# A fused attention and feed-forward kernel: the sign of a decoded weight made on ScalarE, the first batches' normalisations taken from ScalarE to VectorE

## The chip, the core and the metric

The kernel runs on one core of a Trainium2 chip. The metric is the device time of one execution in microseconds (us); lower is better. The engines are named as the profile names them: PE is TensorE (PEld its weight loads), DVE is VectorE, ACT is ScalarE, POOL is GpSimd, SP is SyncE, which here issues nearly all transfers from memory. A name such as L214 is line 214 of the kernel before. In the changed kernel all lines behind L213 have a number that is lower by one.

## The reference

Eight batches with eight heads of a causal attention with a window of 128 and a bias that grows with distance, then a feed-forward layer over all 4608 rows:

```python
scores = scale * np.matmul(q, k.transpose(0, 1, 3, 2))
bias = slopes[:, None, None] * (-np.abs(rel).astype(np.float32))[None, :, :]
mask = (rel >= 0) & (rel < window)
scores = np.where(mask, scores + bias[None], -1000000000.0)
scores = scores - np.max(scores, axis=-1, keepdims=True)
attn = np.exp(scores)
attn = attn / (np.sum(attn, axis=-1, keepdims=True) + 1e-09)
...
h = x @ w_in
g = h * (1.0 / (1.0 + np.exp(-1.702 * h)))
return (g @ w_out).astype(np.float32)
```

Here x is the attention's output laid out as 4608 rows of 512. The weights w_in (512 by 2048) and w_out (2048 by 512) are 64-bit floats.

## The kernel before

**Attention** is worked in units. The batches 0 and 1 are cut into three parts of rows (0 to 256, 256 to 512, 512 to 576) for each pair of heads: these 24 "whole" units (class WholeUnit) work in full float32. The batches 2 to 7 are cut into units that split their operands into a rounded part and a remainder. A unit passes through a pipeline of ticks: load its q, k and v, scores on PE (L325 for whole units), bias and running minimum on DVE (L352), exponentials and row sums on ACT (L375), the reciprocal of the sums on DVE (L393 and L394), the normalisation of the up to four pieces of the unit (L400 and L403), transposes on PE (L420) with copies out of PSUM (L428), and the product with v (L477), copied into the tile xf of a chunk (L486). The scores of one tick need PSUM tiles that DVE's L352 of the tick before has read, and the transposes need all normalised pieces.

**Normalisation of a whole unit.** A string of letters gives the engine of each piece: "PPVA" for the four early units (batch 0, rows 0 to 256), "PAPA" for the others; P is POOL, V is DVE, A is ACT. A unit of 64 rows has two pieces and uses the first two letters. In all there are 36 pieces on ACT, 40 on POOL and 4 on DVE.

**Feed-forward.** The rows are cut into 18 chunks of 256, and for each chunk 16 steps f run over slices of 128 of the 2048 hidden units: 12 products into h_ps (L553), tanh on ACT (L558), the gate on DVE (L559), a rounded part on ACT (L562) and a remainder on POOL (L563), and 6 products into acc (L572). The chunks 0 and 1 run their first steps while the weights are still being decoded: the jobs are chunk 0 with 8 steps, chunk 1 with 16, chunk 0 with its last 8, then the rest.

**Decoding.** A block of 128 by 512 weights arrives as 64-bit words (tile rw, 512 KB, one transfer each, 32 in all, two for each f), and is turned into float32 once. Of each word `top` is the upper half (sign, 11 bits of exponent, 20 of mantissa) and `low` the lower. ACT reads `top` as a float32 and scales it by 2 to the power -112 (L211), which lowers the exponent field so that after a shift left by three the exponent is that of a float32; DVE shifts `low` right by 29 in place (L212), shifts the scaled word left by 3 and joins the three bits from `low` (L213), which drops the sign; then DVE joins the sign bit of `top` (L214). ACT makes the rounded part (L217) and POOL the remainder (L218). The tile `wc` in which the word is made has three buffers, so the L211 of a block waits for the L218 of three blocks earlier. The first eight blocks' instructions are pinned to the program's order.

**What sets the order.** Each engine works through its own list in order. A scheduler sets the lists when the program is built, from its own model of the durations, except where the code pins an order (the transfers on SP's queue, the idle products that open the program at L189, the first eight decodings). Decoding and attention are fed into the feed-forward steps by counters (`owed`, `credit`) that do not depend on measured times. The transfers of weights stand in one queue with those of q, k and v, and these wait for free buffers.

Of the kernel before, what the change touches and what calls it, by code (L numbers as in the profile page):

```python
# [8 lines left out]
F32 = mybir.dt.float32  # L9
# [4 lines left out]
AF = mybir.ActivationFunctionType  # L14
ALU = mybir.AluOpType
# [127 lines left out]
def tile_kernel(ctx: ExitStack, tc: tile.TileContext, q0, k0, v0, qT, kT, v, w_in, w_out, out):  # L143
    nc = tc.nc
# [58 lines left out]
    def decode(st, name, pin=lambda ins: ins):  # L203

        words = st.bitcast(I32).rearrange("p (m two) -> p m two", two=2)
        top, low = words[..., 1], words[..., 0]
        c = ffn.tile([P, 512], I32, name="wc", tag="o", bufs=3)

        pin(nc.scalar.activation(c.bitcast(F32), top.bitcast(F32), AF.Copy, scale=2.0 ** -112))  # L211
        pin(nc.vector.tensor_scalar(low, low, 29, None, ALU.logical_shift_right))  # L212
        pin(nc.vector.scalar_tensor_tensor(c, c, 3, low, ALU.logical_shift_left, ALU.bitwise_or))  # L213
        pin(nc.vector.scalar_tensor_tensor(c, top, -0x80000000, c, ALU.bitwise_and, ALU.bitwise_or))  # L214
        w = c.bitcast(F32)
        res = const.tile([P, 2, 512], F32R, name=name, tag=name)
        pin(nc.scalar.copy(res[:, 0], w))  # L217
        pin(nc.gpsimd.tensor_tensor(res[:, 1], w, res[:, 0].bitcast(F32), ALU.subtract))  # L218
        return res
# [167 lines left out]
    def normal(u):  # L387
        u.rec = att.tile([P, 4], F32, name="rec", bufs=3)
        if u.whole:
            rows, ne = u.blocks[0][1], len(u.p)  # L390
        else:
            rows, ne = u.blocks[0].rows, len(u.blocks)
        nc.vector.tensor_scalar(u.rec[:rows, :ne], u.sums[:rows, :ne], 1e-9, None, ALU.add)  # L393
        nc.vector.reciprocal(u.rec[:rows, :ne], u.rec[:rows, :ne])  # L394
        if u.whole:
            engines = "PPVA" if u.early else "PAPA"
            for _, live, e in u.p:
                rec = u.rec[:rows, e:e + 1]
                if engines[e] == "A":
                    nc.scalar.activation(live, live, AF.Copy, scale=rec)  # L400
                else:
                    on = nc.gpsimd if engines[e] == "P" else nc.vector
                    on.tensor_scalar(live, live, rec, None, ALU.mult)  # L403
            return
        for e, b in enumerate(u.blocks):
            live = b.p[:rows, b.live:b.end]
            nc.vector.tensor_scalar(live, live, u.rec[:rows, e:e + 1], None, ALU.mult)  # L407
# [202 lines left out]
    def tick():  # L610

        nonlocal ticks
        n = ticks

        def stage(k, *steps):
            u = units[n + k] if 0 <= n + k < len(units) else None
            for step in steps:
                if u:
                    step(u)

        stage(1, split_q)
        stage(-2, flip, split_v)
        stage(0, load_v)
        stage(-1, biased)
        stage(1, split_rest)
        stage(-1, exponents)
        stage(-1, normal)
        stage(-2, high, low)
        stage(0, scores)
        stage(-3, mix)  # L630
        if n + 1 < len(units) and units[n + 1] and loads:
            load(loads.pop(0))
        ticks += 1
# [11 lines left out]
    def decode_next():  # L645
        nonlocal halves
        g, ws = halves // 2, (w1, w2)[halves % 2]

        pin = [tc.keep_in_program_order] if halves < PINNED else []
        ws[g] = decode(ws[g], f"w{1 + halves % 2}_{g}", *pin)  # L650
        halves += 1
# [123 lines left out]
```

## Time and profile before

| what | value |
|---|---|
| median of 3 runs | 1074.23 us (1074.23 to 1074.42) |
| profiled execution, from its first to its last instruction | 1072.5 us |
| mean granted PE clock | 0.991 |
| PE busy | 1053.5 us, 98% |
| DVE busy | 687.3 us, 64% |
| ACT busy | 595.2 us, 56% |
| POOL busy | 610.8 us, 57% |

The profile gives no other time of its own execution than this span, 1.7 us below the median of the runs. Its shares are means over stages with different limits. The kernel has a first stage of about 107 us, in which the weights arrive and are decoded beside the whole units, and a long one behind it, in which PE works through prepared operands; the views by stretch of time tell them apart.

### The profile page before, as it was taken

To read this page: it belongs to the slowest core of one execution; us is meant where nothing else is said; L and a number is where in the kernel's file an instruction comes from. 1 tells how busy PE (TensorE), PEld (TensorE's weight loads), DVE (VectorE), ACT (ScalarE), POOL (GpSimd) and SP (SyncE) were. 2 spreads that over 40 slices of the span, in tenths; PEclk is the share of its full clock that TensorE was granted. 3 is DMA by queue.
4 is the path that set the end of the run, shared out by engine and by line. 5 is a ranking of instruction groups with operands and counts; after the bars stand their busy time and mean duration, and the time that the engine had idled before them with its cause. 6 is when DMAs were issued, how large, how long until landed. Compare 5 with 4: busy or idle time off the path is not lost.

```text
span 1072.5 us, 21419 instructions
## 1 busy us (share of the span) xinstructions
PE 1053.5 (98%) x7041; PEld 931.5 (87%) x7041; DVE 687.3 (64%) x2149; ACT 595.2 (56%) x1811; POOL 610.8 (57%) x863
## 2 busy tenths in 40 slices
PE   9888999999999999999999999999999999999998
PEld 5656777899999999999999999999999999999987
DVE  6899843647896777654667668767877687413121
ACT  6869954546665565444555555655665556322222
POOL 3669954556675666554656557656666565323222
PEclk9889999999999999999999999999999999999999
DMA  8861112312223132202222213222222221000000
GB/s 309 305 231 54 44 30 75 83 38 77 75 80 85 51 86 75 62 16 67 58 76 54 70 53 90 75 60 71 82 65 85 57 77 28 20 2 20 1 21 20
DMA packets 88110, 78.45 MB, mean 73 GB/s; under 512 B 36800, under 2 KB 79296, under 8 KB 88000
## 3 DMA queue, kind: packets, MB, share of 16 engines
q1 hardware_dynamic: 82240, 67.14, 21.7%
q10 hardware_dynamic: 5760, 9.96, 2.5%
q8 instruction: 55, 0.90, 0.4%
q14 instruction: 55, 0.45, 0.1%
HBM read 67.63 MB, written 9.44 MB: 72 GB/s over the span
## 4 chain that ended last, share of the span: by engine, by line
PE 92%; DVE 4%; ACT 1%; DMA 1%; issue 0%; POOL 0%; SPq 0%; DVEq 0%; POOLq 0%; ACTq 0%
PE acc L572 37%; PE h_ps L553 37%; PE s_ps L335 5%; PE x_ps L500 5%; PE t_ps L443 4%; PE x_ps L477 1%; DVE wc L214 1%; DVE wc L213 1%; PE t_ps L420 1%; PE sb_ps L325 1%; DVE rw L212 1%; ACT pb L375 1%; PE s_ps L325 1%; DMA rw<-w_out 1%; DVE pb L352 0%; PE acc L189 0%
## 5 line engine op out<-in xcount | busy, mean ns | idle before, releaser
L563 POOL TENSOR_TENSOR gl<-g,gh 128x256 fp32r<-128x256 f32 x288 | 219.7, 763 | 284.1 <-ACT gh L562 220.0
L553 PE MATMUL h_ps<-xh,w 128*128 128x256 f32 x2304 | 370.2, 284 | 1.5 <-DVE g L559 1.0
L553 PEld LDWEIGHTS h_ps<-xh,w 128*128 128x128 f32 x2304 | 329.2, 189 | 33.2 <-DVE g L559 2.0
L572 PE MATMUL acc<-w,gh 128*128 128x512 f32 x1152 | 326.7, 401 | 0.5 <-ACT gh L562 0.5
L558 ACT ACTIVATE g<-h_ps 128x256 f32<-128x256 f32 x288 | 110.0, 382 | 237.5 <-PE h_ps L553 213.3
L559 DVE SCALAR_TENSOR_TENSOR g<-g,h_ps 128x256 f32<-128x256 f32 x288 | 119.4, 415 | 190.6 <-ACT g L558 189.3
L572 PEld LDWEIGHTS acc<-w,gh 128*128 128x128 f32 x1152 | 196.9, 189 | 28.2 <-ACT gh L562 1.1
L553 PE MATMUL h_ps<-xl,w 128*128 128x256 f32 x1152 | 196.1, 281 | 0.0
L562 ACT CAST gh<-g 128x256 fp32r<-128x256 f32 x288 | 116.5, 405 | 137.7 <-DVE g L559 127.0
L572 PE MATMUL acc<-w,gl 128*128 128x512 f32 x576 | 187.6, 401 | 0.1
L553 PEld LDWEIGHTS h_ps<-xl,w 128*128 128x128 f32 x1152 | 165.2, 189 | 6.7 <-issue 0.3
L313 POOL TENSOR_TENSOR K<-rk,K 128x384 fp32r<-128x384 f32 (+1 forms) x120 | 109.1, 909 | 75.0 <-ACT Q L293 14.3
L382 ACT ACTIVATE pb<-pb,mins 128x256 f32<-128x256 f32 (+2 forms) x216 | 105.0, 487 | 40.7 <-DVE mins L363 39.6
L572 PEld LDWEIGHTS acc<-w,gl 128*128 128x128 f32 x576 | 92.6, 189 | 10.5 <-issue 2.2
L407 DVE TENSOR_SCALAR pb<-pb,rec 128x256 f32<-128x256 f32 (+2 forms) x216 | 94.5, 473 | 3.3
L312 POOL TENSOR_TENSOR Q<-rq,Q 64x256 fp32r<-64x256 f32 (+1 forms) x120 | 82.8, 690 | 22.3 <-DVE g L559 3.3
L363 DVE CUSTOM_DVE_ANT_0 pb<-s_ps,bias 128x256 f32<-128x256 f32 (+3 forms) x240 | 85.7, 377 | 11.1 <-PE s_ps L335 9.8
L393 DVE TENSOR_SCALAR rec<-sums 128x2 f32<-128x2 f32 (+3 forms) x144 | 47.7, 331 | 57.6 <-ACT pb L382 52.9
L335 PE MATMUL s_ps<-K,Q 128*128 128x256 f32 (+1 forms) x432 | 80.2, 289 | 0.0
L311 DVE CAST K<-rk 128x384 fp32r<-128x384 f32 (+1 forms) x120 | 51.4, 428 | 44.6 <-PE s_ps L335 39.4
L462 DVE TENSOR_TENSOR pl<-t_ps,ph 128x512 fp32r<-128x512 f32 (+2 forms) x120 | 72.2, 604 | 8.3 <-ACT ph L456 4.5
L443 PE MATMUL t_ps<-ident,pb 128*128 128x128 f32 x408 | 73.9, 272 | 0.0
(69 smaller groups left out, 1354.9 us busy)
## 6 DMA issues: line engine op xcount, KB each, us to landing
rk<-kT SPq DMA_DIRECT2D x72, 192.0 KB, 2.5
rq<-qT SPq DMA_DIRECT2D x96, 128.0 KB, 2.4
out<-o ACTq DMA_DIRECT2D x36, 256.0 KB, 2.1
rw<-w_in SPq DMA_DIRECT2D x16, 512.0 KB, 6.2
rw<-w_out SPq DMA_DIRECT2D x16, 512.0 KB, 7.0
rk<-kT SPq DMA_DIRECT2D x48, 128.0 KB, 2.3
rv<-v SPq DMA_DIRECT2D x96, 64.0 KB, 2.0
rq<-q SPq DMA_DIRECT2D x16, 128.0 KB, 2.2
```

The source lines that it names most:

```text
L313: nc.gpsimd.tensor_tensor(K2, rk, K1.bitcast(F32), ALU.subtract)
L335: nc.tensor.matmul(u.s[:b.rows, e, b.first:b.end], u.Q[:, b.q0 - u.q0:b.q0 - u.q0 + b.rows], k[:, ko:ko + b.end - b.first], start=(z == 0) ...
L363: nc.vector.tensor_tensor_reduce(b.p[ra:rb, cs:b.end], u.s[ra:rb, e, cs:b.end], bias[head][ra:rb, cs:b.end], -SCALE, BIG, ALU.add, ALU.min ...
L382: nc.scalar.activation(live, live, AF.Exp, bias=u.mins[:b.rows, e:e + 1], scale=-1.0, accum_out=u.sums[:b.rows, e:e + 1],)
L407: nc.vector.tensor_scalar(live, live, u.rec[:rows, e:e + 1], None, ALU.mult)
L443: nc.tensor.transpose(u.t[:c.n, w:w + b.rows], b.p[:b.rows, col:col + c.n], ident[:b.rows, :b.rows])
L553: nc.tensor.matmul(h, w1[f][:, z, k * P:(k + 1) * P], x[:, k], start=(n == 0), stop=(n == len(ops) - 1))
L558: nc.scalar.activation(g, h, AF.Tanh, scale=0.851)
L559: nc.vector.scalar_tensor_tensor(g, g, 1.0, h, ALU.add, ALU.mult)
L562: nc.scalar.copy(gh, g)
L563: nc.gpsimd.tensor_tensor(gl, g, gh.bitcast(F32), ALU.subtract)
L572: nc.tensor.matmul(acc, g[:, t * P:(t + 1) * P], w2[f][:, z], start=(f == self.f0 and n == 0), stop=(f == self.f1 - 1 and n == 2))
```

## The change

L211 no longer scales with the function Copy but with Prelu, which multiplies negative values by a further constant `alpha`, here 2 to the power 32. That adds 32 to the exponent field of a negative value, which is one bit of it, and this bit is the one that the shift left by three in L213 moves into the place of the sign. L214 goes. The pieces of the whole units that ACT normalised (L400) are normalised on DVE: "PPVA" becomes "PPVV" and "PAPA" becomes "PVPV". POOL keeps its pieces; only the engine of the others changes, and their order in a unit.

```diff
-        pin(nc.scalar.activation(c.bitcast(F32), top.bitcast(F32), AF.Copy, scale=2.0 ** -112))
+        pin(nc.scalar.activation(c.bitcast(F32), top.bitcast(F32), AF.Prelu, scale=2.0 ** -112, alpha=2.0 ** 32))
         pin(nc.vector.tensor_scalar(low, low, 29, None, ALU.logical_shift_right))
         pin(nc.vector.scalar_tensor_tensor(c, c, 3, low, ALU.logical_shift_left, ALU.bitwise_or))
-        pin(nc.vector.scalar_tensor_tensor(c, top, -0x80000000, c, ALU.bitwise_and, ALU.bitwise_or))
...
-            engines = "PPVA" if u.early else "PAPA"
+            engines = "PPVV" if u.early else "PVPV"
```

Counted over the program, DVE loses 32 instructions at L214 and gains 36 normalisations; ACT loses 36 (L400). Since the scheduler builds the lists anew, many neighbours move too, on all engines but SP, whose list of transfers stays as it was. Two places show it.

The first is on DVE, where it waits for the first half of weight block 7 (rw_7; the number behind a block's name is a counter of the build and differs between the two programs). Before:

```order
L212 TENSOR_SCALAR rw_7_519<-rw_7_519 128x512
L213 SCALAR_TENSOR_TENSOR wc<-wc,rw_2_205 128x512
L393 TENSOR_SCALAR rec<-sums 128x4
L214 SCALAR_TENSOR_TENSOR wc<-rw_2_205,wc 128x512
L212 TENSOR_SCALAR rw_2_207<-rw_2_207 128x512
L394 RECIPROCAL rec<-rec 128x4
L212 TENSOR_SCALAR rw_7_521<-rw_7_521 128x512
L352 ISA pb,mins<-s_ps,bias_76 64x192
L352 ISA mins 64x1
```

The same place in the changed kernel, where L392, L393, L402 and L351 are what L393, L394, L403 and L352 were:

```order
L212 TENSOR_SCALAR rw_7_517<-rw_7_517 128x512
L392 TENSOR_SCALAR rec<-sums 128x4
L393 RECIPROCAL rec<-rec 128x4
L402 TENSOR_SCALAR pb<-pb,rec 128x256 x2
L351 ISA pb,mins<-sb_ps,bias_75 64x192
L351 ISA mins 64x1
L212 TENSOR_SCALAR rw_7_519<-rw_7_519 128x512
L213 SCALAR_TENSOR_TENSOR wc<-wc,rw_3_258 128x512
```

The two steps of the reciprocal, which stood apart with L214 and two other decoding instructions around them, follow each other, the two normalisations that were ACT's stand right behind them, and the decoding of block 2 is done before this place.

The second is on ACT, between the decoding of block 8 and the copies of a 256-row unit's transposes (pw from t_ps). Before:

```order
L217 CAST w_7_948<-wc 128x512
L562 CAST gh<-g 128x256
L400 ACTIVATE pb<-pb,rec 128x128
L400 ACTIVATE pb<-pb,rec 128x256
L428 COPY pw<-t_ps 128x384 x2
L211 ACTIVATE wc<-rw_8_571 128x512
L217 CAST w_8_1030<-wc 128x512
```

The stretch of the changed kernel's list that holds the first copy of that shape, with L374, L427, L216 and L561 for what was L375, L428, L217 and L562:

```order
L374 ACTIVATE pb,sums<-pb,mins 128x128
L374 ACTIVATE pb,sums<-pb,mins 128x256
L427 COPY pw<-t_ps 128x384
L211 ACTIVATE wc<-rw_9_585 128x512
L216 CAST w_9_1083<-wc 128x512
L561 CAST gh<-g 128x256
```

No normalisation stands ahead of the copy any more, and the list has come further in the decoding (block 9 in place of block 8) when it reaches it.

## The prediction

> **What bounds the kernel now.** I read the page's totals first, then the engines' busy time by stretches of time, and then the chain of work that ended last, stretch by stretch.
>
> ```profile
> span 1072.5 us, 21419 instructions
> PE 1053.5 (98%) x7041; PEld 931.5 (87%) x7041; DVE 687.3 (64%) x2149; ACT 595.2 (56%) x1811; POOL 610.8 (57%) x863
> PEclk9889999999999999999999999999999999999999
> ```
>
> ```profile
> core 0: us, PE busy (x) PEld busy (x) DVE busy (x) ACT busy (x) POOL busy (x), PEclk, DMA share, GB/s
> 0.00:32.00 32.00, 28.91 (x191) 18.41 (x193) 22.51 (x94) 22.29 (x71) 12.08 (x23) 1.00 0.88 304
> 32.00:44.00 12.00, 10.76 (x78) 7.45 (x80) 10.34 (x32) 11.51 (x35) 8.46 (x8) 1.00 0.74 239
> 44.00:107.00 63.00, 53.78 (x309) 38.25 (x305) 58.20 (x134) 48.84 (x148) 50.56 (x39) 0.86 0.53 182
> 107.00:200.00 93.00, 93.00 (x590) 72.97 (x589) 49.44 (x130) 60.09 (x192) 58.80 (x62) 1.00 0.19 52
> 47.20:54.10 6.90, 5.95 (x24) 5.13 (x24) 4.00 (x12) 4.60 (x15) 6.90 (x5) 0.51 1.05 399
> 64.30:74.60 10.30, 9.04 (x40) 6.49 (x40) 10.23 (x13) 6.09 (x21) 7.35 (x7) 0.50 0.63 205
> ```
>
> From 107 us on PE is never idle (93.00 of 93.00), and its work is the same in both kernels. So what the change does to the time is what it does to the moment at which PE gets into this steady run. Ahead of it PE loses time in one stage above all, from 44 to 107 us: 63.00 less 53.78, or 9.2 us idle, and 17.2 us (6.90 and 10.30) at half the clock. In this stage DVE is the fullest engine, 58.20 of 63.00. The chain of that stretch says the same:
>
> ```profile
> by line: DVE wc L214 20.4%; DVE wc L213 17.1%; DVE rw L212 13.1%; DVE pb L352 7.2%; DVE rec L393 6.1%; POOL pb L403 5.0%; PE h_ps L553 3.7%; DVE g L559 3.6%; PE acc L572 3.6%; issue 2.9%; DVE xl L539 2.8%; ACT wc L211 2.8%; ACT pb L375 2.6%
> ```
>
> The instruction that goes, L214, is the largest item. The chain of the first 44 us is another one and holds no L214 among its large items; its two longest pieces are transfers of weights:
>
> ```profile
> by line: ACT pb L375 13.2%; DMA rw<-w_out 12.6%; PE acc L189 10.9%; DMA rw<-w_in 10.8%; PE sb_ps L325 9.2%; PE s_ps L325 7.7%; PE x_ps L477 6.8%; PE t_ps L420 6.3%; SPq L155 6.0%; issue 4.0%; ACT pw L428 2.0%; DVE wc L213 1.6%; DVE rw L212
> 26.39 5.56 DMA rw<-w_out
> 38.74 4.76 DMA rw<-w_in
> ```
>
> **The change part by part.** The groups of instructions within 44 to 107 us:
>
> ```profile
> L218 POOL TENSOR_TENSOR w<-wc,w 128x512 fp32r<-128x512 f32 x16 | 23.8, 1491 | 5.1 <-ACT w L217 5.1
> L403 POOL TENSOR_SCALAR pb<-pb,rec 128x256 f32<-128x256 f32 (+2 forms) x14 | 19.6, 1408 | 6.6 <-DVE rec L394 6.6
> L214 DVE SCALAR_TENSOR_TENSOR wc<-rw,wc 128x512 int32<-128x512 int32 x17 | 17.7, 1043 | 0.1
> L211 ACT ACTIVATE wc<-rw 128x512 f32<-128x512 f32 x18 | 12.0, 670 | 0.2 <-POOL w L218 0.2
> L400 ACT ACTIVATE pb<-pb,rec 128x256 f32<-128x256 f32 (+2 forms) x13 | 5.5, 451 | 0.5 <-DVE rec L394 0.5
> ```
>
> *Removed from DVE.* L214 runs 17 times there at 1.04 us, 17.7 us. Of the path it is 20.4% of 63.0, or **12.9 us**; the remaining 4.8 us lie beside ACT, POOL or PE, and I count nothing for them.
>
> *Added to DVE.* The 13 pieces of L400 in this stage become DVE multiplications. The same form ran on DVE only four times before, in the early units:
>
> ```profile
> L214 DVE SCALAR_TENSOR_TENSOR wc<-rw,wc x32: 673/694/2394, 21.9 to 141.3; 128x512 int32<-128x512 int32 x32
> L403 DVE TENSOR_SCALAR pb<-pb,rec x4: 353/408/846, 8.4 to 18.9; 128x256 f32<-128x256 f32 x4
> L403 DVE TENSOR_SCALAR pb<-pb,rec 128x256 f32<-128x256 f32 x4 | 2.0, 504 | 0.1
> L407 DVE TENSOR_SCALAR pb<-pb,rec x216: 279/354/1657, 182.3 to 911.6; 128x256 f32<-128x256 f32 x84, 128x128 f32<-128x128 f32 x12, 128x192 f32<-128x192 f32 x12
> ```
>
> One costs 0.28 us at least (the shortest of the same multiplication at L407, a smaller tile) and 0.85 at most (the longest of the four). I take the mean of the four, 0.504, since its spread already holds the collisions with POOL's halves that start at the same moment: 13 times 0.504 is **6.6 us**, all counted on the path, since the order puts them directly behind the reciprocal and ahead of what DVE does next. The ends are 13 times 0.28, 3.6 us, and 13 times 0.85, 11.1 us.
>
> *Why these durations stretch.* L214 takes 0.67 us when nothing is in its way and 2.39 at worst. Here POOL and DVE hinder each other, in both directions:
>
> ```profile
> 65.45 1.52 POOL L218 TENSOR_TENSOR w<-wc,w 128x512 fp32r<-128x512 f32 x1
> 66.94 0.72 POOL L563 TENSOR_TENSOR gl<-g,gh 128x256 fp32r<-128x256 f32 x1
> ```
>
> ```profile
> 59.33 1.26 DVE L213 SCALAR_TENSOR_TENSOR wc<-wc,rw 128x512 int32<-128x512 int32 x2
> 60.52 0.67 DVE L214 SCALAR_TENSOR_TENSOR wc<-rw,wc 128x512 int32<-128x512 int32 x1
> ...
> 66.01 2.19 DVE L214 SCALAR_TENSOR_TENSOR wc<-rw,wc 128x512 int32<-128x512 int32 x1
> ```
>
> ```profile
> 59.51 4.00 POOL L403 TENSOR_SCALAR pb<-pb,rec 64x192 f32<-64x192 f32 x1 [0.45 <-DVE rec L394]
> ```
>
> From 59.33 us DVE runs one decoding instruction after the other, and POOL's normalisation that starts at 59.51 takes 4.00 us. At 66.01 L214 starts while POOL works, and takes 2.19.
>
> The Trainium skill, "SBUF — State Buffer", section "SBUF: two separate sides", says that a DVE instruction with two SBUF inputs or in a two-port mode and a GpSimd instruction exclude each other for the whole instruction. That speaks partly against the change, since by it a multiplication holds the port as well. The rows above agree. Counted as time on that port, 17 times 0.673 goes and 13 times 0.353 comes, and the sum by the page would be 6.9 us less.
>
> *ACT.* In this stage it loses 5.5 us, with little effect as long as DVE (58.20 of 63.00) is fuller than ACT (48.84); I count 0, and at most these 5.5 us, if ACT is what comes late at the copies behind the normalisations.
>
> *Prelu in place of Copy.* The trace shows no Prelu. L211 takes 0.67 us. The nearest rows are tanh and a plain cast, both on ACT at 128 by 256:
>
> ```profile
> L558 ACT ACTIVATE g<-h_ps 128x256 f32<-128x256 f32 x288 | 110.0, 382 | 237.5 <-PE h_ps L553 213.3
> L562 ACT CAST gh<-g 128x256 fp32r<-128x256 f32 x288 | 116.5, 405 | 137.7 <-DVE g L559 127.0 <-PE acc L572 8.3 <-DVE rec L394 1.4
> L375 ACT ACT_TABLE_LOAD x1 | 1.3, 1283 | 2.6 <-issue 2.6
> ```
>
> They differ by 23 ns, so 46 ns for twice the size, and over 18 blocks 0.8 us to either side, beside DVE's work. I take 0.
>
> *Ahead of 44 us* ten more multiplications move to DVE and four L214 go. The chain there waits on transfers, whose queue keeps its order, so I count 0. Without this cover it is ten times 0.504 less four times 0.67, some 2.4 us lost. *Behind 107 us* PE is busy throughout and covers the rest; 0.
>
> The sum is 12.9 less 6.6, or **6.3 us** less. The profiled span of 1072.5 becomes 1066.2; the median of the runs stands 1.7 us above that span, and 1074.2 becomes **1067.9**. With the ends for a multiplication, 9.3 and 1.8 us less, 1064.9 and 1072.4. What is late next is L213 and L212, still on DVE, and POOL's L218 and L403.
>
> **The rivals.** *More than that: the clock stays up.* The two stretches at half clock lie behind waits of PE in this stage, among them the 4.00 us of POOL above. In the order of the changed kernel DVE reaches the reciprocal earlier behind the arrival of block 7, where PE waits just ahead of the first stretch. PE's busy time there is 5.95 and 9.04 us; at full clock it would be half, 7.5 us less, but PE's lines are only 3.7 and 3.6% of the chain of this stage, 4.6 us, so 2.3 us is what the clock can give at once. With the 9.3 that makes 11.6, or 1062.6. Against it: one remaining wait may be enough to bring the half clock back.
>
> The Trainium skill, "TensorE: Matmul & The Clock Gate", section "What's actually happening", puts the fall to half clock behind an idle window of about 3.4 us. That does not fit this trace in its plain form: no idle time of PE as long as that is in its rows; the longest wait shown for it there is 2.1 us (below). By the page neither stretch should have been, and the clock would have nothing to give.
>
> *No gain: POOL sets the pace.* POOL is busy 50.56 of 63.00 us and keeps all its work. With three buffers for the word being decoded, L211 waits for L218 of three blocks earlier, so a faster DVE only waits there. For it: POOL's fullness. Against it: that wait is 0.2 us now, and POOL's own time includes waiting for DVE (its L403 took 1.41 us on average, 0.60 at the least in the row below). The time would be 1074.2, give or take 2.
>
> *Slower: collisions at each normalisation.* PE's transposes wait for POOL's pieces already:
>
> ```profile
> L403 POOL TENSOR_SCALAR pb<-pb,rec x40: 597/924/3997, 8.6 to 181.3; 128x256 f32<-128x256 f32 x20, 128x128 f32<-128x128 f32 x12, 64x192 f32<-64x192 f32 x8
> PEld t_ps L420 <- POOL pb L403: 5.9, 6, 2.1
> ```
>
> Now DVE's pieces start at the moment POOL's do, released by the same L394, and hold POOL off by 0.35 us each. If POOL's pieces are the last before every transpose and the time of L214 goes unused, 13 times 0.35 is 4.6 us more, or 1078.8. It decides from the point at which PE's wait for POOL's L403 grows by more than the 6.3 us that DVE frees.
>
> *The change does more than it says: Prelu needs another table than the exponential and tanh.* A load takes 1.28 us; two for each of 32 blocks would be 82 us. Against it: the list of ACT has one load in both programs. 1156.
>
> The Trainium skill, "ScalarE activation tables: per-element evaluation and per-set limits", section "What a function is on this engine", has such a switch where two functions are in different sets; no run here shows one.
>
> **How the numbers follow.** The forecast, 1064.9 to 1072.4, has a chance of 0.48; the clock's case 0.24; no gain 0.14; slower by collisions 0.12; table loads 0.02. What a measurement of this kernel can tell from no change is about 0.2%, 2.1 us. Faster by more is the first two, 0.72; within it 0.14; slower 0.14. The range that leaves out no more than 2 in 10 runs from 1060.5 (the clock's case with the unused 2 us of a lighter ACT) to 1076.2 (no gain and 2 us).
>
> **What would show it.** Right: in the stretch up to PE's steady run the chain no longer has L214, DVE's multiplications stand near 0.5 us, PE's idle time falls by some 6 us, and the steady run begins 6 us earlier. Wrong: PE's wait for POOL's normalisations grows beyond 5.9 us, L211 begins to wait for L218, the multiplications take 0.85 us or more, or ACT's list shows L211 longer than 0.75 us. The clock's case shows as a stage without half clock.

## The result, and the profile after

| kernel | median, us | its runs, us | ratio to before, 95% interval |
|---|---|---|---|
| before | 1074.23 | 1073.65 to 1074.42, 4 runs | 1 |
| changed | 1068.45 | 1067.51 to 1069.42, 4 runs | 0.9935, 0.991 to 0.996 |

The change makes the kernel faster by 5.8 us. The profiled execution of the changed kernel took 1067.51 us; its span is 1065.7 where that of before was 1072.5, 6.8 us less. Two far longer runs of the kernel before, of 1694.8 and 2053.5 us among the experiments, are left out of every median and count here. First the page's totals, then its row of the granted clock:

```profile
span 1065.7 us, 21343 instructions
...
PE 1051.5 (99%) x7041; PEld 928.5 (87%) x7041; DVE 674.7 (63%) x2153; ACT 583.1 (55%) x1775; POOL 607.2 (57%) x863
...
PEclk9999999999999999999999999999999999999999
```

PE's busy time is 2.0 us less (1053.5 before), its idle time 4.8 us less (19.0 and 14.2, each the span less the busy time). The engines' busy time by stretches of time, in the stretches of the prediction, with the one stretch at half clock that is left:

```profile
core 0: us, PE busy (x) PEld busy (x) DVE busy (x) ACT busy (x) POOL busy (x), PEclk, DMA share, GB/s
0.00:32.00 32.00, 28.90 (x186) 18.34 (x187) 23.54 (x97) 19.73 (x65) 13.48 (x24) 1.00 0.89 301
32.00:44.00 12.00, 11.96 (x79) 8.13 (x76) 10.89 (x33) 8.85 (x26) 10.02 (x9) 1.00 0.62 191
44.00:107.00 63.00, 56.81 (x362) 40.49 (x361) 58.67 (x143) 51.75 (x162) 54.95 (x46) 0.97 0.59 201
107.00:200.00 93.00, 93.00 (x576) 73.76 (x575) 37.58 (x117) 47.65 (x150) 45.72 (x52) 1.00 0.15 43
54.10:57.50 3.40, 3.40 (x13) 2.29 (x12) 3.37 (x6) 2.11 (x11) 2.27 (x2) 0.50 1.04 367
93.10:107.00 13.90, 13.90 (x88) 10.22 (x89) 10.85 (x31) 13.06 (x41) 13.65 (x13) 1.00 0.25 72
```

In the stage from 44 to 107 us PE is idle for 6.2 us where it was 9.2, and 3.4 us run at half clock where it was 17.2. From 93.1 us on PE never stops. From 32 to 44 us it works 1.2 us more than before (10.76). DVE is as full in the stage as it was, 58.67 and 58.20: what L214 left free has been filled. The chain of waits of this stage, by line and in its four longest DVE pieces (start, length):

```profile
by line: DVE wc L213 23.3%; DVE rw L212 13.5%; PE h_ps L552 10.3%; DVE pb L402 8.7%; DVE pb L351 6.4%; PE acc L571 5.9%; PE x_ps L476 4.0%; issue 3.1%; PE sb_ps L324 2.8%; DVE xl L538 2.8%; DVE g L558 2.6%; PE t_ps L419 2.0%; POOL pb L402 2
...
54.54 2.11 DVE rw L212
...
58.18 2.88 DVE pb L402
...
64.61 3.43 DVE wc L213
...
73.91 2.77 DVE wc L213
```

L214 is gone and L213 has taken its place at the head, with 23.3% where it had 17.1; the new multiplications (L402 on DVE) hold 8.7%. The groups of the stage (count, busy time, mean ns of one, idle time before them):

```profile
L217 POOL TENSOR_TENSOR w<-wc,w 128x512 fp32r<-128x512 f32 x21 | 28.3, 1358 | 1.8 <-ACT w L216 1.5
L213 DVE SCALAR_TENSOR_TENSOR wc<-wc,rw 128x512 int32<-128x512 int32 x21 | 24.3, 1156 | 0.8 <-ACT wc L211 0.8
L402 POOL TENSOR_SCALAR pb<-pb,rec 128x256 f32<-128x256 f32 (+2 forms) x14 | 16.1, 1158 | 6.2 <-DVE rec L393 4.2 <-ACT w L216 1.3 <-ACT wc L211 0.7
L211 ACT ACTIVATE wc<-rw 128x512 f32<-128x512 f32 x20 | 13.5, 677 | 1.0 <-POOL w L217 1.0
L402 DVE TENSOR_SCALAR pb<-pb,rec 128x256 f32<-128x256 f32 (+2 forms) x14 | 8.9, 668 | 0.3
```

21 blocks pass L213 in the stage where 17 did. One L213 takes 1.16 us, where it took 0.84 (17 times, 14.2 us in that group before), and one multiplication 0.668. Two pieces of the timeline, DVE and POOL, show the longest of each:

```profile
57.62 0.86 POOL L402 TENSOR_SCALAR pb<-pb,rec 64x192 f32<-64x192 f32 x1 [1.25 <-DVE rec L393]
58.10 2.95 DVE L402 TENSOR_SCALAR pb<-pb,rec 64x192 f32<-64x192 f32 x1
58.45 2.48 POOL L217 TENSOR_TENSOR w<-wc,w 128x512 fp32r<-128x512 f32 x2
...
63.18 1.82 POOL L402 TENSOR_SCALAR pb<-pb,rec 64x192 f32<-64x192 f32 x1 [0.32 <-DVE rec L393]
64.61 3.42 DVE L213 SCALAR_TENSOR_TENSOR wc<-wc,rw 128x512 int32<-128x512 int32 x1 [0.24 <-ACT wc L211]
64.97 2.50 POOL L217 TENSOR_TENSOR w<-wc,w 128x512 fp32r<-128x512 f32 x2
```

The multiplication that starts at 58.10 ends at 61.05, just behind POOL's two remainders, which end at 60.93; the smaller of DVE's pieces, 64 by 192, takes 2.95 us here. L213 at 64.61 likewise outlasts two remainders (to 67.47). Both start while a normalisation of POOL is still running (to 58.48 and to 65.00). PE's longest waits in this stage, and those for POOL's normalisations, which are down to a fifth of the 5.9 us they were:

```profile
PEld s_ps L324 <- DVE mins L351: 2.0, 2, 1.9
PEld t_ps L419 <- DVE mins L351: 1.9, 1, 1.9
PEld h_ps L552 <- POOL w L217: 1.9, 1, 1.9
PEld t_ps L419 <- POOL pb L402: 1.3, 4, 0.6
```

### The profile page after: what moved, and what is told of

It is laid out like the page before. It is cut to its first block, busy times and chain, and to the rows that moved or that the text cites. A ratio compares the mean times of both kernels' runs of the same rounds, so it can differ in the third digit from the quotient of the medians.

```text
span 1065.7 us, 21343 instructions
## 1 busy us (share of the span) xinstructions
PE 1051.5 (99%) x7041; PEld 928.5 (87%) x7041; DVE 674.7 (63%) x2153; ACT 583.1 (55%) x1775; POOL 607.2 (57%) x863
## 4 chain that ended last, share of the span: by engine, by line
PE 92%; DVE 5%; ACT 1%; DMA 1%; issue 1%; POOL 0%; SPq 0%; DVEq 0%; POOLq 0%; ACTq 0%
PE h_ps L552 37%; PE acc L571 37%; PE s_ps L334 5%; PE x_ps L499 5%; PE t_ps L442 4%; DVE wc L213 2%; PE x_ps L476 1%; PE sb_ps L324 1%; DVE rw L212 1%; PE t_ps L419 1%; DVE pb L402 1%; ACT pb L374 1%; PE s_ps L324 1%; DMA rw<-w_out 1%; DVE pb L351 1%
## 5 line engine op out<-in xcount | busy, mean ns | idle before, releaser
L562 POOL TENSOR_TENSOR gl<-g,gh 128x256 fp32r<-128x256 f32 x288 | 221.7, 770 | 283.4 <-ACT gh L561 226.1
L561 ACT CAST gh<-g 128x256 fp32r<-128x256 f32 x288 | 116.8, 406 | 129.8 <-DVE g L558 122.6
L406 DVE TENSOR_SCALAR pb<-pb,rec 128x256 f32<-128x256 f32 (+2 forms) x216 | 91.0, 458 | 3.2
L392 DVE TENSOR_SCALAR rec<-sums 128x2 f32<-128x2 f32 (+3 forms) x144 | 45.4, 315 | 62.2 <-ACT pb L381 54.0
```

Source lines behind the costliest of these rows:

```text
L561: nc.scalar.copy(gh, g)
L562: nc.gpsimd.tensor_tensor(gl, g, gh.bitcast(F32), ALU.subtract)
```

## The experiments

The twelve experiments are of ten kernels, the changed kernel and the sign alone among them more than once; all compute the whole reference, and the third joins the sign twice. They ran in three series ("calls" in the expectations), each on a chip of its own, with runs of the kernel before in between: its medians were 1077.73 (first series), 1076.51 (second) and 1074.50 us (third). So times are compared within a series, and between series by ratio. Each edit is shown against the kernel before.

**First series: the parts, one at a time**

*The sign alone.*

```diff
-        pin(nc.scalar.activation(c.bitcast(F32), top.bitcast(F32), AF.Copy, scale=2.0 ** -112))
+        pin(nc.scalar.activation(c.bitcast(F32), top.bitcast(F32), AF.Prelu, scale=2.0 ** -112, alpha=2.0 ** 32))
-        pin(nc.vector.scalar_tensor_tensor(c, top, -0x80000000, c, ALU.bitwise_and, ALU.bitwise_or))
```

> Only the first half of the change: Prelu carries the sign, L214 goes, the normalisations stay as before (ACT keeps its 36 pieces). Theory 1 (in the stage of 44 to 107 us DVE's time is what delays PE): the gain is that of L214 alone without the moved multiplications, 9 us (8 to 13), about 1065, and faster than the full change's 1068.5. Theory 2 (half or more of the gain came from the lighter ACT): a gain of 3 us or less, 1071 or more. Theory 3 (the rebuilt lists made the gain, not the removed time): anything, and no shorter DVE chain.

Measured: 1064.14 us (1062.99 to 1064.54), ratio 0.9867 (0.9845 to 0.9888), span 1062.6. Here are the stage's window, then its chain by line, then its group of L213:

```profile
44.00:107.00 63.00, 58.61 (x374) 43.62 (x375) 49.95 (x124) 56.36 (x173) 53.02 (x47) 0.95 0.54 188
```

```profile
by line: PE h_ps L552 22.3%; PE acc L571 18.0%; DVE wc L213 14.7%; DVE rec L392 6.5%; DVE rw L212 6.5%; PE sb_ps L324 6.4%; PE s_ps L324 5.9%; PE t_ps L419 5.8%; PE x_ps L476 5.1%; DVE pb L351 3.3%; issue 2.3%; DVE g L558 2.1%; ACT wc L211 
```

```profile
L213 DVE SCALAR_TENSOR_TENSOR wc<-wc,rw 128x512 int32<-128x512 int32 x20 | 21.4, 1072 | 5.3 <-ACT wc L211 5.2
```

The whole gain is in this part, and more of it than in the full change; the first theory's time is met. DVE is down to 49.95 us of 63.00, and PE's own products head the chain. L213 has grown here too, to 1.07 us: what POOL used to hold up at L214 it now seems to hold up at L213. L212, in turn, got shorter (658 to 545 ns).

*The normalisations alone.*

```diff
-            engines = "PPVA" if u.early else "PAPA"
+            engines = "PPVV" if u.early else "PVPV"
```

> Only the second half: L214 stays, the 36 pieces of the whole units go from ACT to DVE. Theory 1: slower by what the multiplications cost on DVE in the stage, 13 times 0.50 to 0.67 us, that is 6.6 to 8.7 us, about 1081. Theory 2: faster by 3 us or more, 1071 or less, since ACT loses 16 us. In the changed kernel's trace these multiplications took 0.67 us on average in that stage.

Measured: 1083.15 us (1081.77 to 1086.94), ratio 1.0053 (1.0034 to 1.0071). The stage's window, and the group of the moved pieces:

```profile
44.00:107.00 63.00, 53.30 (x309) 38.94 (x309) 60.44 (x135) 44.28 (x136) 52.19 (x38) 0.84 0.56 196
```

```profile
L403 DVE TENSOR_SCALAR pb<-pb,rec 128x256 f32<-128x256 f32 (+2 forms) x12 | 8.2, 706 | 0.1
```

With L214 still there the move costs 0.53%, 5.7 us on that chip, and DVE is fuller than in any other kernel, 60.44. That ACT's relief outweighs the move is refuted.

*Prelu with L214 kept: only the first line of the first diff that is added, in place of the one it replaces.*

> The function of L211 alone: Prelu in place of Copy, while L214 stays and joins the sign a second time (which changes no bit). All lists of instructions are the same as before. If Prelu costs what Copy costs, as the two traces say (L211 0.67 us in both): 1074.2 within 1 us. If part of the change's time were Prelu's own, this shows it: each 0.1 us per block is up to 2 us in the stage.

Measured: 1075.59 us (1073.25 to 1078.68), ratio 0.9978 (0.9961 to 0.9996). The engines' lists are those of before, so this is the price of Prelu: none, or a gain of 0.2% that nothing in the trace explains. Its L211 took 670 ns in the stage, as Copy did. The stage's window:

```profile
44.00:107.00 63.00, 53.92 (x294) 37.84 (x291) 52.91 (x126) 45.45 (x140) 47.58 (x37) 0.81 0.52 179
```

With the same lists the trace of before had DVE busy for 58.20 us, at 0.86 of the clock. So two executions can differ by 5 us in what this window shows, and readings of single traces have that much play.

*The sign by Prelu, and every piece on DVE* (the first diff, with `engines = "VVVV"`).

> The changed kernel with all pieces of the whole units on DVE, those of POOL too (76 of 76). Theory 1 taken by itself (DVE is the bound, so more work on it is slower): 14 more pieces in the stage at 0.35 to 0.67 us, 5 to 9 us, so 1074 to 1078. Rival (POOL and DVE exclude each other, so the sum of both is the bound): POOL's 14 pieces of 1.16 us go, 14 of DVE's at 0.35 come, and DVE's stretched instructions shrink: 16.1 less 4.9 is 11 us less on the shared side, so 1062 to 1066.

Measured: 1075.52 us (1073.97 to 1078.37), ratio 0.9984 (0.9966 to 1.0002). The group of the multiplications in the stage:

```profile
L402 DVE TENSOR_SCALAR pb<-pb,rec 128x256 f32<-128x256 f32 (+2 forms) x24 | 9.3, 436 | 0.1
```

These 24 multiplications keep DVE busy for 9.3 us, hardly longer than the full change's 14 (8.9); POOL has no normalisations left to collide with. And yet all of the gain is lost. So the sum of what DVE and POOL have to do is not what sets the pace. The time is in the first theory's range; that its reason is not the right one either, the eighth run tells.

**Second series: who makes the multiplications long, and which units pay.** All four have the first diff and differ from each other in the string.

*The changed kernel again.*

> The changed kernel once more, on the same chip as the three beside it, so that they can be compared. All theories: 0.9935 of the kernel before, within 0.3%.

Measured: 1067.28 us (1066.81 to 1070.92), ratio 0.9930 (0.9905 to 0.9955): the result repeats.

*20 of the 36 pieces moved:* `engines = "PPVA" if u.early else "PVPA"`.

> Prelu carries the sign; of the 36 pieces that the change took from ACT, 20 go to DVE and 16 stay on ACT (PPVA for the early units as before, PVPA for the others). Theory 1 (each multiplication on DVE in the stage costs its 0.5 to 0.7 us): 7.4 us lay between the sign alone and the full change for 14 pieces in the stage; here about 9 of the 14 move, so 4.8 us above the sign alone and 2.6 below the full change, a ratio to before near 0.991. Rival (what decides is whether the lists are laid well): no order by number of moved pieces, outside of the two kernels it stands between.

Measured: 1068.23 us (1067.45 to 1069.21), ratio 0.9927 (0.9905 to 0.9950). Moving fewer is no cheaper that one could measure: the ratio is that of the full change, but the interval holds the first theory's 0.991 too, so this run does not decide between the two. DVE's groups:

```profile
L213 DVE SCALAR_TENSOR_TENSOR wc<-wc,rw 128x512 int32<-128x512 int32 x21 | 19.4, 922 | 4.1 <-ACT wc L211 4.1
...
L402 DVE TENSOR_SCALAR pb<-pb,rec 64x192 f32<-64x192 f32 (+2 forms) x9 | 4.3, 474 | 0.1
```

Both are shorter than in the full change (1156 and 668), though POOL has 14 normalisations in the stage here as well.

*The later units' pieces shared by DVE and ACT, none on POOL:* `engines = "PPVA" if u.early else "VAVA"`.

> Prelu carries the sign; ACT keeps its pieces as before, and POOL's pieces of the units behind the early ones go to DVE (VAVA; the early units stay PPVA). Theory 1 (DVE's own time is the bound): about 12 pieces more on DVE in the stage at 0.35 to 0.67 us, 4 to 8 us above the sign alone, ratio 0.991 to 0.994. Rival (DVE and POOL exclude each other, and the sum of both is the bound): 12 pieces of 1.0 us leave the shared side and 12 of 0.35 come, so up to 7.8 us below the sign alone, ratio 0.980 to 0.985.

Measured: 1069.44 us (1067.66 to 1070.46), ratio 0.9935 (0.9912 to 0.9958). The window ahead of the stage, the stage's window and DVE's groups:

```profile
32.00:44.00 12.00, 9.15 (x42) 6.31 (x39) 10.25 (x33) 8.85 (x27) 3.32 (x3) 0.73 0.60 195
44.00:107.00 63.00, 59.41 (x377) 42.74 (x376) 52.67 (x140) 55.70 (x171) 40.37 (x32) 0.97 0.58 194
```

```profile
L213 DVE SCALAR_TENSOR_TENSOR wc<-wc,rw 128x512 int32<-128x512 int32 x20 | 16.3, 829 | 1.0 <-ACT wc L211 1.0
...
L402 DVE TENSOR_SCALAR pb<-pb,rec 128x256 f32<-128x256 f32 (+2 forms) x14 | 5.5, 420 | 0.1
```

The same number of multiplications as in the full change, 14, takes 5.5 us in place of 8.9, and L213 is back at 0.83 us. So POOL's normalisations have a part in what stretches DVE's instructions in the changed kernel. How large a part is not shown: the kernel with 20 pieces moved keeps them and is nearly as short (922 and 474), and two kernels without any in the stage, the one with all pieces on DVE and the one that follows, have L213 at 932 and 915 and a multiplication at 436 and 548. The total doesn't hang on it: DVE has 6.0 us less to do in the stage (52.67 for 58.67), and the kernel is not faster. The ratio is in the first theory's range, and the rival's 0.980 to 0.985 is refuted. It loses elsewhere: from 32 to 44 us PE is busy for 9.15 us at 0.73 of the clock, where it was 11.96 at full clock in the changed kernel.

*The four early pieces on DVE as in the change, all later ones on DVE too:* `engines = "PPVV" if u.early else "VVVV"`.

> The changed kernel with POOL's pieces on DVE too, but only those of the units behind the early ones (VVVV; the early units as in the changed kernel, PPVV). The run with all pieces on DVE was 0.4 to 0.5% slower than the change, and its half clock began at 32 us, with longer waits of PE in the early units. If it was the early units that lost it, this one is at the change's time or below (ratio 0.990 to 0.994). If it was DVE's load in the stage, it is as slow as that run (0.997 to 0.999).

Measured: 1066.78 us (1066.32 to 1068.55), ratio 0.9915 (0.9890 to 0.9941), with 28 multiplications of 0.548 us in the stage. It differs from the kernel with all pieces on DVE in two pieces of each of the four early units, which POOL keeps here. So that kernel lost its 0.7% by moving these eight pieces at the very start, and not by DVE's load in the stage. The time itself is for the most part lost later. The stage's window of the kernel with all pieces on DVE, then of this one:

```profile
44.00:107.00 63.00, 58.21 (x329) 41.83 (x327) 56.25 (x135) 49.53 (x145) 43.66 (x32) 0.86 0.54 193
```

```profile
44.00:107.00 63.00, 57.05 (x364) 41.68 (x363) 59.35 (x148) 51.40 (x155) 41.03 (x33) 0.95 0.57 198
```

DVE is fuller here, and the clock higher. Counted as in the table further down, the spans' difference of 9.3 us falls with 1.1 ahead of 32 us, 0.4 from there to 44, 4.8 in the stage and 3.0 behind it.

**Third series: the price of the move, and where it falls.** On one chip: the sign alone, the full change, and the move of the four early or of the 32 later pieces alone (`"PPVV"` with `"PAPA"`, and `"PPVA"` with `"PVPV"`).

> The sign alone, as in the first experiment, now beside the full change on the same chip. Theory 1 (VectorE sets the pace of the stage from 44 to 107 us; the 13 multiplications that the change puts there cost 13 x 0.668 us = 8.7 us of VectorE's time, of which part lies beside idle moments): faster than the full change by 3 to 7 us, that is a span of some 1061 to 1064 us where the full change's is 1065 to 1068. Rival (the gap between the two in earlier calls was the chip's clock, not the multiplications): within 1.5 us of the full change at the same mean granted clock.

> The changed kernel again, as the yardstick of this call: both theories expect a ratio of 0.991 to 0.996 against the kernel before and a time between 1066.5 and 1071 us, by the granted clock of the run.

> The sign by Prelu, and only the four early pieces' normalisation moved from ScalarE to VectorE; the 32 later ones stay on ScalarE. Theory 1 (what the multiplications cost is paid in the stage from 44 to 107 us, by the later units): like the sign alone, within 1 us of it. Rival (the early units pay, since VectorE is wanted most before TensorE runs without gaps): like the full change, 3 us or more above the sign alone.

> The sign by Prelu, and only the 32 later pieces' normalisation moved; the four early ones stay on ScalarE. Theory 1: like the full change, within 1 us of it, and 3 us or more above the sign alone. Rival (the early units pay): within 1 us of the sign alone.

| kernel | median, us | its runs, us | ratio, 95% interval | span, us |
|---|---|---|---|---|
| sign alone | 1066.08 | 1064.04 to 1067.05, 6 | 0.9904, 0.9877 to 0.9931 | 1064.9 |
| full change | 1068.32 | 1067.01 to 1069.83, 6 | 0.9931, 0.9906 to 0.9956 | 1065.9 |
| early pieces moved | 1067.56 | 1065.69 to 1068.24, 6 | 0.9920, 0.9895 to 0.9944 | 1066.0 |
| later pieces moved | 1070.30 | 1068.92 to 1072.11, 12 | 0.9949, 0.9933 to 0.9965 | 1070.3 |

The sign alone beats the full change by 2.2 us: less than the 3 expected, more than the 1.5 of the rival. The intervals of the ratios overlap, but of the 36 pairs of a run of the one and a run of the other 35 have the sign alone ahead. The later pieces alone cost 4.2 us, as the first theory had it, but 2.0 more than the full change, which it had not; the early pieces alone cost 1.5, which lies between. So neither theory is met in full.

To see where these few us go, I took for each product of PE the time from its start to the start of the next, and subtracted the median of its kind behind 150 us (over all kernels). The sum over a stretch is what PE lost there on the same work, waits and half clock together; it is below zero ahead of 32 us, since products run closer there than the typical ones later. Only differences between rows mean anything. For the six traces with Prelu the sums differ as their spans do, to 0.1 us; the kernel before takes 1.0 us longer than they from PE's last product to the end of the program (5.3 and 4.4 us).

| kernel | 0 to 32 us | 32 to 44 | 44 to 107 | behind 107 | sum |
|---|---|---|---|---|---|
| before | -3.8 | 0.0 | 18.0 | 5.2 | 19.4 |
| full change, first result | -3.0 | -0.1 | 9.5 | 7.3 | 13.6 |
| full change, third series | -3.0 | 0.2 | 9.5 | 7.1 | 13.8 |
| sign alone, first series | -4.0 | 1.2 | 6.7 | 6.6 | 10.5 |
| sign alone, third series | -3.7 | 3.1 | 6.8 | 6.6 | 12.8 |
| early pieces moved | -3.0 | 4.5 | 5.5 | 6.9 | 13.9 |
| later pieces moved | -3.0 | -0.6 | 13.9 | 7.8 | 18.2 |

Each taken as the mean of its two rows, the full change loses 0.9 us ahead of 32 us against the sign alone, gains 2.1 from 32 to 44, loses 2.8 in the stage and 0.6 behind it; two traces of the sign alone differ by as much as 1.9 in one stretch. The gain from 32 to 44 us has a row in PE's waits there. The sign alone, third series, and then the early and the later pieces moved:

```profile
PE sb_ps L324 <- ACT pw L427: 1.1, 1, 1.1
```

```profile
PE sb_ps L324 <- ACT pw L427: 1.1, 1, 1.1
```

```profile
PE sb_ps L324 <- ACT pw L427: 0.3, 1, 0.3
```

PE waits for ACT's copy of the transposes as long as ACT normalises the later pieces, and hardly where it doesn't (the 0.3 is at 30.0 us). The wait isn't the whole of the difference: in the window of the sign alone, third series, the clock is down as well, which it isn't in the trace of the first series (1.00).

```profile
32.00:44.00 12.00, 9.86 (x57) 6.28 (x56) 9.73 (x27) 10.15 (x30) 7.12 (x7) 0.86 0.71 219
```

The kernel before has the same wait, 1.2 us, and the full change has none. The move of the early pieces brings one of 1.0 us on the same copy at 19.5 us, in the full change and with the early pieces alone; neither the kernel before nor the sign alone has it.

What the later pieces alone lose beyond the full change, 4.4 us in the stage, is mostly half clock. The stage's window in these two, the later pieces first, then the full change of the third series:

```profile
44.00:107.00 63.00, 57.33 (x334) 41.37 (x334) 56.04 (x130) 47.81 (x147) 49.02 (x43) 0.86 0.54 184
```

```profile
44.00:107.00 63.00, 57.96 (x361) 41.48 (x362) 58.53 (x145) 51.84 (x162) 54.87 (x46) 0.95 0.57 198
```

PE is about as busy, but at 0.86 of the clock in place of 0.95: half clock holds for 6.8 and 10.2 us of the stage in place of 6.8 in all, and 10.2 us at half clock are 5.1 us of work. Why the clock falls there and not in the full change, these runs do not settle.

## Why the prediction was right, step by step

The direction and the place were right, and so was the size, but the size in part by luck: two terms were too large by about as much, and much of what came was the clock's, which the sum had not counted.

**Only the stage counts: nearly.** By the table PE loses 8.5 us less in the stage, of 5.8 in all. The rest is small and of both signs: 0.8 more ahead of 32 us and 2.1 more behind 107 us, where PE is "busy" in both kernels but works less closely. The cover of 93.00 of 93.00 busy was not a full one. (With the 1.0 us behind PE's last product, the 5.8 are the 6.8 by which the spans differ.)

**L214 removed, 12.9 us: the right term, too large.** The sign alone takes 9.9 and 7.6 us off the span (1072.5 to 1062.6 and 1064.9), and 8.4 us off the median of before in the third series and 13.6 in the first, where the kernel before ran slower. Two things were left out. L213 inherits a part of L214's collisions: a block took 842 and 1043 ns before and takes 1072 without L214, so it saves 0.81 us and not 1.04; 12.9 times 0.81 over 1.04 is 10.0 (an estimate, which leaves out that L212 got shorter too). And PE's own products then head the chain, as its row shows; L213 and L212, which the prediction named as next, come behind them.

**Thirteen multiplications, 6.6 us: too small as work, too large as cost.** There were 14 in the stage, at 0.668 us and 8.9 us busy in all, above the forecast and within its end of 0.85. But not "all counted on the path": the full change costs 2.2 us beyond the sign alone in the series that has both (4.3 between the medians of the first result and the first series, on different chips). What failed is the addition. With L214 in place the move costs 5.7 us (3.7 to 7.6 by the interval of the ratio), close to the forecast. Without L214 DVE is idle for 13.0 us of the stage (63.00 less 49.95; 10.9 in the trace of the third series), and of 8.9 us of multiplications the table has 2.8 as lost there. That the idle time takes up the rest fits these figures, but no run tests it alone. A rival stands: each edit lays the lists anew, and this can be worth as much. With the four early pieces moved as well, the kernel with the later pieces moved gets 2.0 us faster, and eight early pieces more cost the kernel with all pieces on DVE 0.7%. The two terms were worked out against the same full DVE, and each was too large by a similar amount: the removal by some 3 to 5 us, the addition by some 4. That these errors cancel is why the sum, 6.3, came within half a us of the measured 5.8, and it is luck.

**ACT's relief, 0: right against the kernel before.** PE's idle time from 32 to 44 us falls from 1.2 us to 0.0, but by the table, in which the products' closeness counts too, before and the full change are level there (0.0 and -0.1). The loss of 2.4 that the prediction feared in this stretch did not come. Against the sign alone the move is worth something there: that kernel loses 1.2 and 3.1 us, partly in PE's wait for ACT's copy, and the larger of the two partly at half clock. In the stage nothing shows that ACT's relief helped, as forecast.

**Prelu as Copy, 0: right.** 677 ns against 670 in the stage, a ratio of 0.9978 for Prelu alone, and one load of a table in the list of ACT, as before.

**The rivals.** *POOL sets the pace:* L211's wait for L217 rose to 1.0 us from 0.2, and POOL is at 54.95 of 63.00, but the blocks still came faster, 21 in place of 17. One wait of 1.9 us on POOL's remainder (L217) stands among PE's longest now. *Collisions:* they were there, and as the prediction said DVE's pieces fall on POOL's; but DVE is the one held off, with a piece of up to 2.95 us, while POOL's normalisations got shorter (1408 to 1158 ns) and PE's wait for them fell from 5.9 to 1.3 us. *The clock:* in part. The half clock fell by 13.8 us. PE was busy for 14.99 us of it before (5.95 and 9.04) and for 3.40 after; half of the difference, 5.8 us, is what the clock gave, more than the 2.3 that the chain's share was read to allow. The idle time fell by 3.0, half the forecast "some 6 us". Together these are 8.8, near the table's 8.5 for the stage. So about two thirds of the gain there came through the clock and one third through the waits themselves; the prediction had the clock as a case of its own, and its sum held only the other.

**What was to show it.** L214 gone from the chain: yes. Multiplications near 0.5 us: no. L211's wait, named as a sign against it, did begin (1.0 us) and did not stop the gain. The steady run was to start 6 us earlier: PE's last wait ended at 106.4 us before and at 93.0 after, 13.4 us earlier, of which the end saw 6.8. The moment of the last wait is no measure of the time.

## What to carry to other kernels

An instruction taken off the fullest engine and one put on it need not add up, and here they did not: price the second in the profile that the first leaves behind, where another engine may head the chain. The best version here is the half of the change that only removes work, the sign alone: 1064.14 and 1066.08 us. When an instruction goes that another engine was colliding with, look at which neighbour inherits the collision before counting its whole mean.

## What was not expected of the hardware

**The kernel before has no single time.** Its 53 runs in the three series follow the mean granted clock: of 25 at 0.991 to 0.995 all but two took 1072.6 to 1075.8 us (those two 1076.3 and 1077.5), and 28 at 0.985 to 0.990 took 1076.8 to 1081.3. The changed kernel has the same on a smaller scale: in the second series four runs at 0.998 took 1066.81 to 1067.31 us and two at 0.993 took 1070.56 and 1070.92. What decides it stays open. It is most of why the sign alone gained 13.6 us in one series and 8.4 in another: the medians of before differ by 3.2 us there, its own by 1.9.

**Half clock without a long wait.** In the changed kernel PE's longest wait in the stage is 1.9 us, and half clock begins at 54.1 us, 0.9 us behind a wait of 1.6. The Trainium skill, "TensorE: Matmul & The Clock Gate", section "What's actually happening", has an idle window of about 3.4 us ahead of it; no wait of this length is in the stage in any trace of this case (the longest is 2.5 for a product and 3.1 for a weight load, with the normalisations alone moved). The stretches at half clock themselves are 3.4, 6.8 or 10.2 us long, and in the trace of Prelu with L214 kept one is 23.9.

**DVE and POOL hold each other off for more than one instruction.** The Trainium skill, "SBUF — State Buffer", section "SBUF: two separate sides", has an exclusive lock on a shared pair of ports, which an instruction keeps to its end. The rows at 58.10 and 64.61 us agree that one waits for the other, and go further: DVE's instruction starts there during a normalisation of POOL, and ends only behind two remainders that POOL starts later than it. The other way round, POOL's normalisation of 4.00 us in the kernel before lies beside a row of DVE's decoding instructions. So an engine whose instructions follow each other closely kept the other out over several of them, in both directions. The run without POOL's later normalisations has L213 at 829 ns in place of 1156 and a multiplication at 420 in place of 668; as the other experiments show, the presence of these normalisations is not all that decides it.
